# The short token set's first products moved into a long set's pass, with buffers and the pace of weight making laid out anew

## Chip, cores and metric

One core of a Trainium2 chip runs the whole program in one launch. The metric is the device time of one execution in microseconds (us); less is better. The engines: TensorE (PE in the rows; PEld is its weight load) multiplies, VectorE (DVE) and ScalarE (ACT) do elementwise work, GpSimd (POOL) a little of it, SyncE (SP) issues nearly all transfers. SBUF is the working memory, PSUM the eight banks of 512 float32 per partition that TensorE writes.

## What is computed

The reference, cut: kernel attention over 4 x 8 heads of 576 tokens, then two gated layers on the 2304 token rows of width 512, with a hidden width of 1536.

```python
def phi(x):
    h = np.einsum('bhsd,md->bhsm', x, omega) - np.sum(x * x, axis=-1, keepdims=True) / 2.0
    return np.exp(h - np.max(h, axis=-1, keepdims=True)) / np.sqrt(m)
q_p, k_p = phi(q * scale), phi(k * scale)
kv, z = np.einsum('bhsm,bhsd->bhmd', k_p, v), np.sum(k_p, axis=2)
x = np.einsum('bhsm,bhmd->bhsd', q_p, kv) / (np.einsum('bhsm,bhm->bhs', q_p, z)[..., None] + 1e-06)
x = x.transpose(0, 2, 1, 3).reshape(2304, 512)
g = x @ w_gate;  x = (g / (1 + np.exp(-g))) * (x @ w_val) @ w_out              # layer 1
x = (1 / (1 + np.exp(-(x @ w_gate2)))) * (x @ w_val2) @ w_out2                 # layer 2
```

The six layer weights come as float64 and are made float32 on the chip.

## The kernel before

**Attention** runs first (to about 165 us), pair of heads by pair, in an order written out by hand (`ORDER`). It leaves x transposed in `xx`: 512 features on partitions and blocks, 2304 tokens along the free axis. Of these 2048 are the long part (512 of each batch) and 256 the short one (`TAIL`, 64 of each batch).

**The layers.** Each layer handles three token sets: long set 0 and long set 1 of 1024 tokens (`big(l, n, ...)`), then the short set of 256 (`rest(l)`). A set has a first stage (x times w_gate and w_val, then the gate) and a second (hidden times w_out). Every product is three matmuls (`three`): each operand is split into a high and a low float32r part (xhi, xlo for x; vh, vl for a weight; hh, hl for the hidden values), the high part by a ScalarE copy, the low part by a VectorE subtraction.

**First stage of a long set.** The 12 hidden column blocks are done in 6 pairs `p`. A pair takes seven products in a Winograd form, `k` = 0 to 6, of the operands B11, T1, T2, B21, T3, B22, T4 (the T are differences of quarters of x, made by `x_sum`). Product k uses weight tile `w` of its slot, 12 matmuls of 512 columns, and lands in PSUM pair X, Z, X, Y, X, Z, X. X gathers k = 0, 2, 4 and 6 by accumulation, so that between them ScalarE copies it out (k = 0 and 2, `copy`), VectorE adds it to a temporary (k = 4, `total`, tiles p5 and u2), and after k = 6 `gate` reads it last. X alternates between two pairs of banks (`next_x`).

**Weights.** A unit (a 128 x 512 block) is loaded as float64 (raw), made float32 by one ScalarE operation (magnitude, L150) and four on VectorE (bits, power, term, total: L158 to L179), summed with its neighbours for the seven forms (`sums`, wsums, L224), and stored in DRAM (wf, ws). From there `fetch` reads each tile when its turn in `sequence` comes, three steps ahead (`AHEAD`), and `prepare` splits it (vh L314, vl L318). The 36 units of layer 1 must be made while attention and the first pass run: 12 are made inside attention (`early`), the others by the generator `make`, of which `step` takes a few turns after each product: as many as the weight `room` of that step and the next due time in `needs` ask for (`SHARES` scales this by stage).

**The short set** (`rest`) comes after the two long ones of its layer, with two weight tiles of two slots (0 and 3, or 6 and 7) for each hidden block, which it fetches and splits again, 24 tiles, and 12 of w_out: 36 tiles of 12 (layer 2's w_out: 6) matmuls each.

Engines run their own queues in order; waits are semaphores. TensorE's order in a long set's pair is the order of k, and behind it come the ready tile's steps. Lines that the text names: L261 `x_sum`, L271 and L274 `x_split` (xlo, xhi), L329 to L331 `three`, L870 and L871 `gate`, L878 and L879 `split` (hh, hl), L884 `copy`, L889 `total`, L896 `evict`.

Of the kernel before, what the change touches and what calls it, by code (L numbers as in the profile page):

```python
# [28 lines left out]
Q_ON_VECTOR = True  # L29
EARLY_SPLITS = 10  # L30
# [3 lines left out]
SHARES = (1, 1.5, 1, 1, 0.5), (1.2, 1.5, 1, 1, 1), 1  # L34
CALM = ()
MARGIN = 1
ENDS_BY = 1
NEGATIVE = -(2.0**32)
# [3 lines left out]
def tile_performer_attention__then__two_glu_layers(  # L42
# [170 lines left out]
    def sums(u, v, t):  # L213
# [17 lines left out]
        "T1": ("B12", "B11", 0),  # L231
        "T2": ("B22", "T1", 1),
        "T3": ("B22", "B12", 0),
        "T4": ("B21", "T2", 1),
    }
    xc, xt, fetched, ready = {}, {}, {}, {}
    sequence = []
    for l in range(2):
        for n in range(2):
            sequence += [("f", l, p, s) for p in range(FC // 2) for s in SLOT7]  # L240
            sequence += [("s", l, c) for c in range(FC)]
        for c in range(FC + 2):
            if c < FC:
                sequence += [("f", l, c // 2, s) for s in ((0, 3), (6, 7))[c % 2]]
            if c >= 2:
                sequence.append(("s", l, c - 2))

    def in_rest(o):
        return o % (len(sequence) // 2) >= 2 * (7 * FC // 2 + FC)

    def x_part(s, name):
        if name[0] == "T":
            return xt[name]
        k, ab = 2 * (name[1] == "2"), 2 * s + (name[2] == "2")
        return xx[:, k:k + 2, ab * TS:(ab + 1) * TS]

    def x_sum(s, name, later):
        l, r, place = SUMS[name]

        t = xt["T2"] if name == "T4" else temporary((("s0", "s1"), ("u2", "p5"))[later][place], "xt")  # L260
        nc.vector.tensor_tensor(t, x_part(s, l), x_part(s, r), ALU.subtract)  # L261
        xt[name] = t

    def x_split(s, i, low):
        k, kk = divmod(i, 2)
        tag = f"w{2 * RING + 2 * i + low}"
        t = wres.tile([P, TS], F32R, tag=tag, name="xlo" if low else "xhi")
        src = x_part(s, ORDER7[k])[:, kk]
        if low:
            hi = xc[k, kk][0]  # L270
            nc.vector.tensor_tensor(t, src, hi.bitcast(F32), ALU.subtract)  # L271
            xc[k, kk] = hi, t
        else:
            nc.scalar.activation(t, src, AF.Copy)  # L274
            xc[k, kk] = (t,)
# [15 lines left out]
    def fetch(o):  # L291
        if o < len(sequence) and o not in fetched and o not in ready:
            kind, l, c, *slot = sequence[o]
            if in_rest(o) and o % 6 > 3:
                t = temporary(("u2", "p5")[o % 2], "wp", shape=(P, 2 * H2))
# [3 lines left out]
            if kind == "s":  # L299
# [55 lines left out]
    with ExitStack() as st:  # L355
# [352 lines left out]
        early = [(n, units.pop(0)) for n in range(len(pairs) + 1) if n % 3 < 2]  # L708
# [9 lines left out]
        for (_, ua), (n, ub) in zip(early[::2], early[1::2]):  # L718
# [13 lines left out]
        def begin(i):  # L732
            if i == 0:
                begun.append(next_x())
# [33 lines left out]
    xs, tmp = pool("xs", 1), pool("tmp", 1)  # L768
    rows = out.rearrange("(b s) e -> b s e", s=S)
# [15 lines left out]
    def make():  # L785
# [3 lines left out]
        for _ in range(2):  # L789
            yield  # L790
# [39 lines left out]
    for at, (kind, l, *_) in enumerate(sequence):  # L830
        phase = at % (len(sequence) // 2)
        tail = phase >= 2 * 54
        share = SHARES[l][4 if tail else 2 * (phase // 54) + (phase % 54 >= 42)]
        if l == 0 and at < 7:
            share *= SHARES[2]
        if phase < 108 and phase % 54 in CALM:
            share *= 0.1
        room.append(share * (0.53 if tail else 1 + (kind == "s")))
    needs, turns = [], 3
# [12 lines left out]
    def step(n):  # L852
# [4 lines left out]
        prepare(o + AHEAD)  # L857
        o += 1
# [8 lines left out]
    def gate(l, h, src):  # L867
# [3 lines left out]
        after(1, lambda: nc.vector.tensor_tensor(h, g, src[1], ALU.mult))  # L871
# [14 lines left out]
    def total(l, h, left, t):  # L886

        for i in range(2):
# [217 lines left out]
```

## Time and profile before

| | |
|---|---|
| time, median of 3 runs | 1012.7 us (1012.38 to 1017.41) |
| the profiled execution | 1014.05 us, of which the span from first to last instruction is 1012.3 |
| PE busy | 989.5 us (98% of the span), 5497 matmuls |
| PEld, DVE, ACT, POOL busy | 844.2, 722.1, 595.8, 35.9 us |
| DMA | 167.54 MB moved, 53.1% of the engines' time in the queue that SyncE issues |

A busy matmul row lasts longer than the distance to the next one, since matmuls are pipelined; so the distance between starts is what counts, and idle time shows only where TensorE waited for something. Where VectorE or ScalarE is idle, nothing is lost unless TensorE waits for it later.

### The profile page before, as it was taken

What the parts mean: (1) busy time and instruction counts of PE and PEld (TensorE: products, weight loads), DVE (VectorE), ACT (ScalarE), POOL (GpSimd) and SP (SyncE); (2) the same over time, 40 slices, a digit from 0 to 9 for tenths busy, and PEclk for the clock granted to TensorE, in tenths of its full rate; (3) what the DMA queues carried; (4) which work ended last, traced back from release to release, by engine and by line L of the source; (5) the groups of instructions that cost most, each with busy time, mean ns of one, the idle gap of its engine ahead of it and who ended that gap; (6) DMA issues with size and microseconds to landing.
All of it is one profiled execution on the core that took longest, in us unless ns stands there. A gap on an engine that the chain in (4) does not pass through costs nothing.

```text
span 1012.3 us, 15829 instructions
## 1 busy us (share of the span) xinstructions
PE 989.5 (98%) x5497; PEld 844.2 (83%) x5497; DVE 722.1 (71%) x1465; ACT 595.8 (59%) x1259; POOL 35.9 (4%) x58
## 2 busy tenths in 40 slices
PE   7999999799999999999999999999999999999998
PEld 6999998588878888888789998888888888888897
DVE  6899998899988977678677757767553554553364
ACT  7999998455654465545456565565345545533454
POOL 2222220000000000000000000000000000000000
PEclk9999999799999999999999999999999999999999
DMA  7656866688875566665445666664114333321463
GB/s 211 166 155 171 219 178 184 193 281 295 276 228 156 158 202 182 189 188 176 132 126 186 218 206 206 204 192 143 52 53 136 102 96 92 105 55 50 166 197 96
DMA packets 136404, 167.54 MB, mean 166 GB/s; under 512 B 32260, under 2 KB 89604, under 8 KB 136324
## 3 DMA queue, kind: packets, MB, share of 16 engines
q1 hardware_dynamic: 134740, 163.65, 53.1%
q0 software_dynamic: 1584, 2.88, 1.7%
q8 instruction: 43, 0.70, 0.3%
q14 instruction: 37, 0.30, 0.1%
HBM read 127.43 MB, written 36.18 MB: 162 GB/s over the span
## 4 chain that ended last, share of the span: by engine, by line
PE 85%; DVE 7%; ACT 2%; issue 2%; DMA 1%; SPq 1%; DVEq 0%; ACTq 0%
PE X L329 14%; PE X L331 14%; PE X L330 14%; PE Z L329 6%; PE Z L331 6%; PE Z L330 6%; PE Y L331 5%; PE Y L329 5%; PE Y L330 5%; PE p L536 3%; PE o L590 2%; PE o L616 2%; PE o L602 1%; PE t L498 1%; DVE vl L318 1%
## 5 line engine op out<-in xcount | busy, mean ns | idle before, releaser
L318 DVE TENSOR_TENSOR vl<-wp,vh 128x512 fp32r<-128x512 f32 x288 | 197.5, 688 | 146.6 <-ACT vh L314 144.0
L314 ACT ACTIVATE vh<-wp 128x512 fp32r<-128x512 f32 x288 | 177.5, 623 | 14.2 <-PE Y L331 4.8
L329 PE MATMUL X<-xhi,vh 128*128 128x512 f32 x384 | 150.9, 393 | 7.4 <-DVE p L889 7.4
L330 PE MATMUL X<-xlo,vh 128*128 128x512 f32 x384 | 150.6, 392 | 0.3 <-DVE xlo L271 0.3
L331 PE MATMUL X<-xhi,vl 128*128 128x512 f32 x384 | 150.6, 392 | 0.0
L329 PEld LDWEIGHTS X<-xhi,vh 128*128 128x128 f32 x384 | 72.8, 190 | 23.1 <-issue 7.7
L879 DVE TENSOR_TENSOR hl<-h,hh 128x1024 fp32r<-128x1024 f32 (+1 forms) x56 | 49.3, 880 | 58.7 <-ACT hh L878 58.5
L330 PEld LDWEIGHTS X<-xlo,vh 128*128 128x128 f32 x384 | 72.8, 189 | 15.8 <-DVE xlo L271 0.7
L331 PEld LDWEIGHTS X<-xhi,vl 128*128 128x128 f32 x384 | 72.7, 189 | 15.4 <-DVE vl L318 0.2
L878 ACT ACTIVATE hh<-h 128x1024 fp32r<-128x1024 f32 (+1 forms) x56 | 43.5, 777 | 68.6 <-PE X L330 39.1
L329 PE MATMUL Z<-xhi,vh 128*128 128x512 f32 x192 | 75.0, 390 | 0.1
L330 PE MATMUL Z<-xlo,vh 128*128 128x512 f32 x192 | 74.8, 390 | 0.0
L331 PE MATMUL Z<-xhi,vl 128*128 128x512 f32 x192 | 74.8, 389 | 0.0
L331 PE MATMUL X<-xr,vl 128*128 128x256 f32 x192 | 54.3, 283 | 0.0
L329 PE MATMUL X<-xr,vh 128*128 128x256 f32 x192 | 54.2, 282 | 0.0
L330 PE MATMUL X<-xr,vh 128*128 128x256 f32 x192 | 54.2, 282 | 0.0
L150 ACT ACTIVATE mag<-raw 128x512 f32<-128x512 f32 x72 | 48.1, 673 | 6.7 <-DVE res L179 2.1
L171 DVE SCALAR_TENSOR_TENSOR mag<-raw,mag 128x512 f32<-128x512 uint32 x72 | 50.7, 704 | 1.2
L884 ACT ACTIVATE Y<-X 128x512 f32<-128x512 f32 x48 | 27.8, 584 | 35.9 <-PE X L331 35.4
L274 ACT ACTIVATE xhi<-xt 128x512 fp32r<-128x512 f32 x32 | 19.9, 630 | 47.2 <-DVE xt L261 47.2
L870 ACT ACTIVATE g<-u 128x512 f32<-128x512 f32 x24 | 15.2, 633 | 54.8 <-DVE u L889 54.8
L870 ACT ACTIVATE g<-p 128x512 f32<-128x512 f32 x24 | 15.2, 632 | 52.9 <-DVE p L889 52.9
(170 smaller groups left out, 2388.3 us busy)
## 6 DMA issues: line engine op xcount, KB each, us to landing
wp<-wf SPq DMA_DIRECT2D x216, 256.0 KB, 3.1
wp<-ws SPq DMA_DIRECT2D x72, 256.0 KB, 2.8
raw<-in_moe_w_gate_dram SPq DMA_DIRECT2D x24, 512.0 KB, 4.6
raw<-in_moe_w_val_dram SPq DMA_DIRECT2D x24, 512.0 KB, 4.8
wf<-res SPq DMA_DIRECT2D x48, 256.0 KB, 3.5
wf<-wsums SPq DMA_DIRECT2D x48, 256.0 KB, 3.6
raw<-in_moe_w_out_dram SPq DMA_DIRECT2D x24, 512.0 KB, 4.4
ws<-res SPq DMA_DIRECT2D x24, 256.0 KB, 3.8
```

Source lines behind the costliest of these rows:

```text
L150: nc.scalar.activation(self.mag, self.hi.bitcast(F32), AF.Prelu, scale=REBIAS, alpha=NEGATIVE)
L171: nc.vector.scalar_tensor_tensor(self.mag, self.lo, 2.0**-52, self.mag, ALU.mult, ALU.mult)
L314: nc.scalar.activation(hi, fetched[o], AF.Copy)
L318: nc.vector.tensor_tensor(lo, fetched.pop(o), hi.bitcast(F32), ALU.subtract)
L329: nc.tensor.matmul(o, lhsT=l[0], rhs=r[0], start=start, stop=False, **kw)
L330: nc.tensor.matmul(o, lhsT=l[0], rhs=r[1], start=False, stop=False, **kw)
L331: nc.tensor.matmul(o, lhsT=l[1], rhs=r[0], start=False, stop=stop, **kw)
L536: nc.tensor.matmul(pj[a][:, i, :], lhsT=x[hs, i, :], rhs=wdf[hs, a, :], start=True, stop=True)
L870: nc.scalar.activation(g, src[0], AF.Sigmoid if l else AF.Silu)
L878: nc.scalar.activation(hi, src, AF.Copy)
L879: nc.vector.tensor_tensor(lo, src, hi.bitcast(F32), ALU.subtract)
L884: nc.scalar.activation(d, s, AF.Copy)
```

## The change

`rest` is gone. The short set's first products run inside one long pass of each layer (layer 1: long set 0; layer 2: long set 1), on the weight tile that the step has in hand: `slots` marks slots 0, 3 and 7 of a pair as also used by the short set (12 matmuls of 256 columns more, `small_first`), and adds a step for slot 6, whose tile only the short set uses. In the pair p = 0 only slot 7 is shared, and slots 0, 3 and 6 follow as three steps of their own. So the program takes 256 weight tiles where it took 288; the number of matmuls stays. The short products land in a bank pair of their own (R, banks 4 and 5; one bank for both halves of a hidden block), and in these passes X stays on banks 0 and 1 instead of alternating. The short set's second products follow at once after that long set's second products.

SBUF: the temporaries p5 and u2 go; the copies of Z and X land in the hidden tiles themselves (h2, h1 and the next pair's h). The T differences live in the x operands' own tiles. The short set's split x and every second split of hidden blocks (hh, hl with odd c) share the tags xh and xl.

Weight making: a turn's room is now 2.74 times the step's products less 0.6 times an estimate of VectorE's work there, near nothing in the last slots of the last pair; the first 7 steps get a fifth; the last early pair's four sums move from attention into `make`. ScalarE's table loads for Silu and Sigmoid are asked for ahead by a one-element activation (`table`).

```diff
+LEAD = 3
+EARLY_UNITS = 12
+FULL = (4, 5, 6, None)
+SPENT = 0.6
+LEFT_OVER = 1
-SHARES = (1, 1.5, 1, 1, 0.5), (1.2, 1.5, 1, 1, 1), 1
+SHARES = ((1, 1, 1, 1), (1, 1, 1, 1), 0.2, 7)
+LATE_START = (7,)
+SMALL_AT = 7
...
+    LARGE = (0, 0, True), (0, 1, False), (1, 0, False), (1, 1, True)
+    REST = {0: (0, 0), 3: (0, 1), 7: (1, 1), 6: (1, 0)}
+    def slots(l, n, small, p):
+        ks = [(s, k, small and s in REST) for k, s in enumerate(SLOT7)]
+        if small and p == 0:
+            ks = [(s, k, s in LATE_START) for s, k, _ in ks]
+            return ks + [(s, None, True) for s in (0, 3, 7, 6) if s not in LATE_START]
+        return ks + [(6, None, True)] * small
...
+                full = p == FC // 2 - 1 and product in FULL
+                vector.append(9 if full else 0.6 + {4: 1.8, 5: 1.8, 6: 0.6, None: 0.6}.get(product, 0))
...
+        left_over = [(a[1], b[1]) for a, b in couples[len(couples) - LEFT_OVER:]]
...
-        room.append(share * (0.53 if tail else 1 + (kind == "s")))
+        room.append(share * max(2.74 * x - SPENT * y, 0.1))
...
         prepare(o + AHEAD)
+        while soon:
+            soon.pop(0)()
...
-            temporary(f"s{2 * low + c % 2}", "h" + "hl"[low], F32R, src.shape)
+            temporary((f"s{low}", "x" + "hl"[low])[c % 2], "h" + "hl"[low], F32R, src.shape)
...
+    def table(f):
+        nc.scalar.activation(tiny[:, 1:], tiny[:, :1], f)
...
+    def small_first(kh, w, bank, start, stop):
+        for n in range(2):
+            for kk in range(2):
+                fs = slice(n * H2 + kk * P, n * H2 + (kk + 1) * P)
+                three(
+                    bank[:, n * R:(n + 1) * R],
+                    [u[:, fs] for u in w],
+                    [u[:, 2 * kh + kk] for u in small_x],
...
-            X, Y = begun or (next_x(), banks(3, "Y"))
+            X, Y = begun or (banks(0, "X") if small else next_x(), banks(3, "Y"))
...
+                if r and k == 0:
+                    small_step()
...
                 if k == 1:
-                    copy([p5[:, i] for i in range(2)], Z)
+                    copy(h2, Z)
+                    if early:
+                        table(AF.Silu)
                 if k == 2:
-                    copy([u2[:, i] for i in range(2)], X)
+                    h[2 * p + 2] = h_tile(2 * p + 2)
+                    u2 = h[2 * p + 2][:, 0] if p < FC // 2 - 1 else h[2 * p + 2][0]
+                    u2 = [u2, h1[1]]
+                    copy(u2, X)
...
                 if k == 6:
-                    after(1, partial(gate, l, h2[0], X))
+                    after(1, partial(gate, l, h2[0], X, small))
+                if r and k != 0:
+                    small_step()
...
-                    hs[c] = split(h[c], c)
+                    after(1 + (c == 0), partial(lambda c: hs.update({c: split(h[c], c)}), c))
+        if small:
+            acc = [ps.tile([P, MAIN], F32, tag=f"b{i}", name="acc") for i in (6, 7, 2, 3, 4, 0, 1, 5)]
...
+            elif small and c + 2 == FC:
+                small_hi_lo(0)
...
-        rest(0)
```

**How the order moves: three places.** VectorE's queue in pair p = 0 of the first pass, before, from the low split of slot 4's tile (vl) to the adds after k = 4. In the names, res and mag are a unit being made, xt the T difference (here T4), X and p5 the PSUM pair and the temporary of `total`.

```order
L318 TENSOR_TENSOR vl_3224<-wp_2917,vh_3223 128x512
L171 SCALAR_TENSOR_TENSOR mag_3196<-raw64_3172,mag_3196 128x512
L179 TENSOR_TENSOR res_3198<-res_3198,mag_3196 128x512
L158 TENSOR_SCALAR res_3235<-mag_3233 128x512
L261 TENSOR_TENSOR xt_2471<-xx_76,xt_2471 128x1024
L271 TENSOR_TENSOR xlo_3252<-xt_2471,xhi_3250 128x512
L271 TENSOR_TENSOR xlo_3256<-xt_2471,xhi_3254 128x512
L318 TENSOR_TENSOR vl_3261<-wp_3170,vh_3260 128x512
L165 TENSOR_SCALAR mag_3233<-res_3235 128x512
L171 SCALAR_TENSOR_TENSOR mag_3233<-raw64_3174,mag_3233 128x512
L179 TENSOR_TENSOR res_3235<-res_3235,mag_3233 128x512
L158 TENSOR_SCALAR res_3273<-mag_3271 128x512
```

The same stretch of the change, from two xlo ahead of slot 3's tile to the adds; h stands where p5 stood.

```order
L304 TENSOR_TENSOR xlo_3123<-xt_3068,xhi_3109 128x512
L304 TENSOR_TENSOR xlo_3135<-xt_3068,xhi_3121 128x512
L352 TENSOR_TENSOR vl_3165<-wp_2555,vh_3164 128x512
L352 TENSOR_TENSOR vl_3186<-wp_2738,vh_3185 128x512
L230 TENSOR_TENSOR wsums_3195<-res_3074 128x256
L304 TENSOR_TENSOR xlo_3215<-xx_76,xhi_3213 128x512
L304 TENSOR_TENSOR xlo_3219<-xx_76,xhi_3217 128x512
L352 TENSOR_TENSOR vl_3222<-wp_2919,vh_3221 128x512
L295 TENSOR_TENSOR xt_2472<-xx_76,xt_2472 128x512 x2
L304 TENSOR_TENSOR xlo_3243<-xt_2472,xhi_3241 128x512
L304 TENSOR_TENSOR xlo_3247<-xt_2472,xhi_3245 128x512
L352 TENSOR_TENSOR vl_3252<-wp_3168,vh_3251 128x512
```

The res and mag rows are gone from this stretch (five ahead of T4, four behind), three of four wsums have moved behind it, and slot 3's vl now stands behind two xlo that it preceded.

VectorE's queue at the end of the first pass (pair p = 5), before, from the adds after k = 5 to the last gate product, which frees the pair X.

```order
L889 TENSOR_TENSOR u2_4181<-Z_4180,u2_4181 128x512
L871 TENSOR_TENSOR xx_76<-g_4307,p5_4182 128x512
L318 TENSOR_TENSOR vl_4336<-wp_4256,vh_4335 128x512
L171 SCALAR_TENSOR_TENSOR mag_4285<-raw64_4231,mag_4285 128x512
L179 TENSOR_TENSOR res_4315<-res_4315,mag_4285 128x512
L879 TENSOR_TENSOR hl_4348<-h_3163,hh_4347 128x1024
L871 TENSOR_TENSOR xx_76<-g_4333,u2_4181 128x512
L318 TENSOR_TENSOR vl_4368<-wp_4279,vh_4367 128x512
L158 TENSOR_SCALAR res_4373<-mag_4345 128x512
L165 TENSOR_SCALAR mag_4345<-res_4373 128x512
L171 SCALAR_TENSOR_TENSOR mag_4345<-raw64_4281,mag_4345 128x512
L871 TENSOR_TENSOR xx_76<-g_4365,X_4176 128x512
```

The same of the change.

```order
L939 TENSOR_TENSOR xx_76<-Z_4515,xx_76 128x512
L929 TENSOR_TENSOR hl_4695<-h_3158,hh_4694 128x1024
L915 TENSOR_TENSOR xx_76<-g_4672,xx_76 128x512
L352 TENSOR_TENSOR vl_4702<-wp_4603,vh_4701 128x512
L915 TENSOR_TENSOR xx_76<-g_4699,xx_76 128x512
L929 TENSOR_TENSOR hl_4733<-h_3159,hh_4732 128x1024
L352 TENSOR_TENSOR vl_4739<-wp_4644,vh_4738 128x512
L915 TENSOR_TENSOR xx_76<-g_4736,X_4511 128x512
L352 TENSOR_TENSOR vl_4761<-wp_4678,vh_4760 128x512
L915 TENSOR_TENSOR hr_4757<-g_4758,R_4517 128x256
```

No res or mag row stands there any more; both hl stand ahead of the product that frees X, and behind it comes the short set's last gate product, which frees R.

ScalarE's queue at the same place of the change, from the gate after k = 5.

```order
L912 ACTIVATE g_4699<-u2_4596 128x512
L348 ACTIVATE vh_4701<-wp_4603 128x512
L928 ACTIVATE hh_4732<-h_3159 128x1024
L912 ACTIVATE g_4736<-X_4510 128x512
L348 ACTIVATE vh_4738<-wp_4644 128x512
L912 ACTIVATE g_4758<-R_4517 128x256
L348 ACTIVATE vh_4760<-wp_4678 128x512
```

hh_4732 takes over the memory of the short set's split x (tag xh), so that it waits for TensorE's last short product of the pass, and the gate on X now stands behind it.

## Rows read from the trace of the kernel before

**Rows 1.** which engine TensorE waited for, whole span: us in total, times, longest
```profile
PE X L329 <- DVE p L889: 7.4, 1, 7.4
PE X L329 <- DVE xx L871: 2.6, 2, 2.4
```

**Rows 2.** stages: busy us (x instructions) of PE, PEld, DVE, ACT, POOL; clock, DMA
```profile
183.30:195.90 12.60, 5.26 (x13) 4.14 (x14) 10.02 (x18) 7.00 (x12) 0.00 (x0) 0.60 0.42 125
195.90:291.20 95.30, 95.30 (x422) 78.93 (x421) 90.48 (x170) 56.62 (x102) 0.00 (x0) 1.00 0.85 275
...
362.20:476.40 114.20, 114.20 (x505) 94.62 (x504) 81.41 (x146) 64.42 (x115) 0.00 (x0) 1.00 0.60 182
...
543.80:595.40 51.60, 51.60 (x434) 51.57 (x433) 36.28 (x72) 31.02 (x66) 0.00 (x0) 1.00 0.76 247
595.40:956.40 361.00, 361.00 (x1586) 297.42 (x1585) 199.78 (x301) 179.00 (x298) 0.00 (x0) 1.00 0.39 117
```

**Rows 3.** timeline of TensorE, pair p = 0: start us, us, what [idle before]
```profile
175.15 0.50 PE L331 MATMUL Y<-xhi,vl 128*128 128x512 f32 x1 [0.25 <-DVE vl L318]
...
182.89 0.39 PE L331 MATMUL Z<-xhi,vl 128*128 128x512 f32 x1
190.63 0.76 PE L329 MATMUL X<-xhi,vh 128*128 128x512 f32 x1 [7.35 <-DVE p L889]
...
195.89 0.44 PE L329 MATMUL X<-xhi,vh 128*128 128x512 f32 x1
```

**Rows 4.** timeline of VectorE, pair p = 0
```profile
174.41 0.68 DVE L318 TENSOR_TENSOR vl<-wp,vh 128x512 fp32r<-128x512 f32 x1
175.01 0.42 DVE L224 TENSOR_TENSOR wsums<-wsums,res 128x256 f32<-128x256 f32 x1
175.35 0.68 DVE L271 TENSOR_TENSOR xlo<-xt,xhi 128x512 fp32r<-128x512 f32 x1
...
177.83 0.42 DVE L158 TENSOR_SCALAR res<-mag 128x512 uint32<-128x512 uint32 x1
...
178.62 1.28 DVE L271 TENSOR_TENSOR xlo<-xx,xhi 128x512 fp32r<-128x512 f32 x2
...
182.09 1.22 DVE L261 TENSOR_TENSOR xt<-xx,xt 128x1024 f32<-128x1024 f32 x1
184.00 1.29 DVE L271 TENSOR_TENSOR xlo<-xt,xhi 128x512 fp32r<-128x512 f32 x2 [0.69 <-ACT xhi L274]
186.95 0.69 DVE L318 TENSOR_TENSOR vl<-wp,vh 128x512 fp32r<-128x512 f32 x1 [1.65 <-ACT vh L314]
...
189.80 1.29 DVE L889 TENSOR_TENSOR p<-X,p 128x512 f32<-128x512 f32 x2
```

**Rows 5.** timeline of ScalarE, pair p = 0
```profile
173.34 0.68 ACT L150 ACTIVATE mag<-raw 128x512 f32<-128x512 f32 x1
...
183.34 1.15 ACT L274 ACTIVATE xhi<-xt 128x512 fp32r<-128x512 f32 x2 [6.13 <-DVE xt L261]
184.51 1.28 ACT L870 ACT_TABLE_LOAD   x1
185.80 0.60 ACT L870 ACTIVATE g<-Y 128x512 f32<-128x512 f32 x1
```

**Rows 6.** timeline of TensorE, end of the first pass
```profile
295.83 0.40 PE L331 MATMUL X<-hh,vl 128*128 128x512 f32 x1
298.62 0.80 PE L329 MATMUL X<-hh,vh 128*128 128x512 f32 x1 [2.39 <-DVE xx L871]
...
301.77 0.42 PE L330 MATMUL X<-hl,vh 128*128 128x512 f32 x1
```

**Rows 7.** timeline of VectorE, end of the first pass
```profile
294.02 1.22 DVE L879 TENSOR_TENSOR hl<-h,hh 128x1024 fp32r<-128x1024 f32 x1
...
297.88 0.68 DVE L871 TENSOR_TENSOR xx<-g,X 128x512 f32<-128x512 f32 x1
```

**Rows 8.** timeline of ScalarE, end of the first pass
```profile
292.52 1.04 ACT L878 ACTIVATE hh<-h 128x1024 fp32r<-128x1024 f32 x1
```

More of the change, by code (lines that the diff above doesn't have):

```diff
@@ L273, in x_split @@
         else:
+            t = wres.tile([P, TS], F32R, tag=x_tag(k, kk, 0), name="xhi")
             nc.scalar.activation(t, src, AF.Copy)
@@ L707, in tile_performer_attention__then__two_glu_layers @@
         }
-        early = [(n, units.pop(0)) for n in range(len(pairs) + 1) if n % 3 < 2]
+        early = [n for n in range(len(pairs) + 1) if n % 3 < 2][:EARLY_UNITS]
+        early = [(n, units.pop(0)) for n in early]
         for name in "load", "magnitude", "bits", "power", "term", "total":
@@ L768, in tile_performer_attention__then__two_glu_layers @@
     xs, tmp = pool("xs", 1), pool("tmp", 1)
+    tiny = tmp.tile([P, 2], F32, name="tiny")
+    nc.vector.memset(tiny, 0.0)
     rows = out.rearrange("(b s) e -> b s e", s=S)
@@ L788, in make @@
             u.load()
-        for _ in range(2):
-            yield
+        for u, v in left_over:
+            t = []
+            yield from sums(u, v, t)
+            put(u, v, t)
         todo = None
@@ L829, in tile_performer_attention__then__two_glu_layers @@
     room = []
[L830 to L834, printed above, removed]
+    for (kind, l, *_), x, y in zip(sequence, weight, vector):
+        second = sum(z[0] == "s" and z[1] == l for z in sequence[:len(room)]) >= FC
+        share = SHARES[l][2 * second + (kind != "f")]
+        if len(room) < SHARES[3]:
             share *= SHARES[2]
-        if phase < 108 and phase % 54 in CALM:
-            share *= 0.1
-        room.append(share * (0.53 if tail else 1 + (kind == "s")))
-    needs, turns = [], 3
+        room.append(share * max(2.74 * x - SPENT * y, 0.1))
+    needs, turns = [], 1 + 4 * LEFT_OVER
     for i, u in enumerate(units):
@@ L886, in total @@
     def total(l, h, left, t):
-        for i in range(2):
-            nc.vector.tensor_tensor(t[:, i], left[i], t[:, i], ALU.add)
-        after(1, lambda: gate(l, h, [t[:, i] for i in range(2)]))
+        for x, y in zip(left, t):
+            nc.vector.tensor_tensor(y, x, y, ALU.add)
+        after(1, lambda: gate(l, h, t))
+    def table(f):
+        nc.scalar.activation(tiny[:, 1:], tiny[:, :1], f)
     def evict(n, dst, src):
@@ L902, in big @@
         own = slice(n * 2 * TS, (n + 1) * 2 * TS)
+        if small:
+            held = [tmp.tile([P, i, R], F32, tag=f"hr{at}", name="hr") for at, i in enumerate(HELD[:-1])]
         def h_tile(c):
+            if c == FC:
+                return [wres.tile([P, TS], F32, tag=x_tag(0, 0, 0), name="u2")]
             if c < 8:
@@ L942, in big, with small_hi_lo @@
                     c = (k - 3) // 2
-                    hs[c] = split(h[c], c)
-        acc = [next_x(), banks(3, "Y"), banks(1, "Z"), next_x()]
-        acc = [t for pair in acc for t in pair]
+                    after(1 + (c == 0), partial(lambda c: hs.update({c: split(h[c], c)}), c))
+        if small:
+            acc = [*Y, *Z, R2[0], *X, R2[1]]
+            acc = [ps.tile([P, MAIN], F32, tag=f"b{i}", name="acc") for i in (6, 7, 2, 3, 4, 0, 1, 5)]
+        else:
+            acc = [t for pair in (next_x(), banks(3, "Y"), banks(1, "Z"), next_x()) for t in pair]
         todo = [f for _, f in following]
-        for _ in range(2):
+        for _ in range(3):
             clock += 1
             run()
+        if l == 0 and n == 1:
+            table(AF.Sigmoid)
+        hr = {}
+        def small_hi_lo(i):
+            hr[i] = split(held[i], i)
         for c in range(FC):
@@ L973, in big @@
             store(dst, t[:, b % 2])
[L975 to L992 removed]
+        if not small:
+            return
         Y = banks(3, "Y")
         acc = [t[:, j * R:(j + 1) * R] for t in Y for j in range(2)] if l == 0 else Y
[L995 to L1005 removed]
         def second(c, w, js=range(4 - 2 * l)):
+            i, at = place_of(c)
+            now = [u[:, at] for u in hr[i]]
             for j in js:
```

213 lines of the change are left out of this document (114 added, 99 removed).

## The prediction, made before the changed kernel ran

> **What bounds the kernel now.** First the stages, to see which engine is full in each: TensorE is busy for all of 195.9 to 291.2, 362.2 to 476.4, 543.8 to 595.4 and 595.4 to 956.4 [rows 2]. There its own pace sets the time, and what other engines save is worth nothing. That pace is the distance between starts: 114.2 us for the 504 matmuls of a long first stage, 0.2267 us each at 512 columns (one row of the 505 is the next stage's), and 51.6 for 434 in the short set, 0.119 each at 256 [rows 2]. Then the list of who waits: in the layers TensorE waited 7.4 us once for the adds on X, and 2.6 us twice for the gate product on X, the longer time 2.4, so the other 0.2 [rows 1]. Third, the timeline at both places. At the first the next matmul starts at 190.63 instead of 183.12, and then the next twelve start 0.44 apart on average, not 0.2267, until 195.89 [rows 3]: the granted clock of 183.3 to 195.9 is 0.60 [rows 2], that is, 1.2 GHz for part of it and not 2.4. At the second it starts at 298.62 instead of 296.06, again with the lower clock behind it, until 301.77 [rows 6]. All that can be won in the layers is there: 7.5 + 2.5 and 2.6 + 1.6, and 0.2, some 14.4 us.
>
> **Why TensorE waits at 183.** X is freed by the adds at 189.80. VectorE was never idle before T4's difference at 182.09: it had the weight making, the sums and the splits to do in order [rows 4]. T4 ended at 183.3; then came ScalarE's high splits, a table load of 1.28, a gate, slot 6's vh [rows 5], and VectorE's xlo, vl (late at 186.95), four making operations, the adds [rows 4].
>
> **The change, step by step.** The sum is made against the profiled execution, 1014.05 us with a span of 1012.3; the median of the runs is 1012.7, and I take the difference from that.
>
> *Matmuls: 0.* Their number and shapes stay. 576 short products cost 0.119 each before, and I take the same when they alternate with long ones; the bounds are half a long one's 0.2267, 0.0057 less, which is -3.3 us, and as much more, +3.3.
>
> *32 weight tiles fewer: 0.* Transfer, vh and vl of the short set lie under TensorE, which is busy for all 51.6 us of its stage [rows 2]; VectorE there has 36.3. Without that cover a tile would cost VectorE the 0.69 of a vl [rows 4].
>
> *Opening (p = 0).* Ahead of T4 VectorE loses five making operations: 177.83 to 182.09 is 4.26, less an xlo pair 1.2 and a vl 0.6 that stay, 2.45; and three of four sums, 0.34 each (175.01 to 175.35), 1.0 [rows 4]. It gains some 0.1 for a memset and a second instruction of T4. So T4 ends at 183.3 - 3.35 = 179.95. Then the high splits (0.55 each), the gate on Y and slot 6's vh (0.5 each) take ScalarE to 181.7 with no table load between [rows 5]; vl ends at 182.3, one sum at 182.65, the first add at 183.25, the second at 183.85. One step gets later: slot 3's vl, for which TensorE waited 0.25 at 175.15 [rows 3], now stands behind two xlo (+1.2) and one sum fewer (-0.35) and the memset (+0.1): TensorE stops 1.2 instead of 0.25 and ends k = 5 at 184.05 instead of 183.12. Then X is free and k = 6 goes at once, 12 x 0.2267 = 2.7, done at 186.8 where it was 195.89 [rows 3]: **-9.1**. The table load moves to k = 1, where ScalarE loses two magnitude operations of 0.68 [rows 5] for its 1.28: 0 net, and slot 5's splits hide it. Bounds: none of the lower clock, or 1.2 us of idle time calling it for as long as 2.4 did [rows 6], 1.6 lost; or the fall of 3.35 alone helps, the first rival.
>
> The load took 1.28 us, and the next activation began 0.01 after it [rows 5]. The Trainium skill (ScalarE: Activation LUTs, "What ACT_TABLE_LOAD costs") says that a switch costs some 2.66 us, since 1.38 of draining comes on top of the load; the trace does not agree. By the page slot 5's splits and T4 would come about 1 us later in the new place, and the sum below would be -12.0.
>
> *Pair 0 to 1.* The three added steps last 12 x 0.119 = 1.43 each, and pair 1 begins with a short product on R, whose gate and product come only a step earlier. VectorE's queue from the adds on (two xr, seven splits, adds and gate products at 0.6, two sums) brings R free at about 192.7; TensorE is there at 192.5. **+0.3**; 0 to 1.2 (a gate product and a vl more).
>
> *The rest of the first pass.* VectorE was busy 90.5 of 95.3 us there [rows 2], nearly full. Now the stage has 24 uses of 12 short products, 34 us more of TensorE, for at most 15 us of VectorE (8 vl, 12 gate products, a split of x): 0.
>
> *End of a short-carrying pass.* Before, 2.6 + 1.6 were lost here, because the product that frees X stood behind making operations and an hl [rows 7]. The making is gone from the stretch. A new wait comes: hh_4732 waits for the last short product, and behind it on ScalarE stand the gate on X and on R, on VectorE hl, vl and both products. From that product's end: hh 1.04, hl 1.2, vl 0.6, product 0.6 and hand-overs [rows 4, 7, 8], some 3.6. The second products begin on six other banks' worth, so that X's second bank is wanted after 6 x 3 x 0.2267 = 4.1, R's after 4.8, and R comes 4.7 to 4.9 after. **-4.1** for layer 1's old stop, **+0.2** for both layers together; 0 to 1.0.
>
> *Short second stage.* The third hh takes the place of the first, so it waits for product 3; hh, hl and vl need at most 2.9 before product 6, and products 4 and 5 give 2.9. **+0.1**, 0 to 0.6. Stores and the end stay as they were.
>
> *Second pass, layer 1.* Little making is left in its last slots either: **-0.2** of the 0.2.
>
> Sum: -9.1 + 0.3 - 4.1 + 0.2 + 0.1 - 0.2 = -12.8. The profiled execution would take 1001.3, and the median 1012.7 - 12.8 = **999.9 us**.
>
> **The rivals.**
>
> *The opening is only shortened.* If the chain behind T4 keeps its length (a late transfer, another operation ahead of the adds), only the 3.35 of T4 is won, the idle time stays at 4 us and the lower clock with it: -3.35 - 4.1 + 0.3 = 1005.5. For it: the chain had two other waits, on vh and xhi [rows 4]. Against it: table load and four making operations leave the chain too.
>
> *Slower: one pair X.* In the short-carrying passes X no longer alternates, so k = 0 of the next pair waits for the gate product after k = 6. From X's last matmul there are 2 x 1.43 of short products, 1.43 more ahead of k = 0, and 1.36 for X's first bank: 5.65. Before, at the end of the first pass, that product ended at 298.5, 7.3 after 291.2 [rows 2, 7]. Were it as late at each of ten boundaries, each would cost 1.65 and some lower clock, as much again: 33, less the 12.8, so 1033. It decides from 1.3 a boundary. Against it: the chain itself is 0.5 + 0.6 + 0.6, the lateness was making's, and in layer 2's pass VectorE is little loaded (199.8 of 361 [rows 2]).
>
> *No change: given back later.* The first 7 steps make a fifth as much, and pair 3's tiles wait for their units; the 12.8 returns as stops for a tile: 1012. Against it: the first pass's 34 us against 15 above.
>
> **How the numbers follow.** The forecast, with the bounds of its terms, 0.70; the opening only shortened 0.13; one pair X, 0.08; given back 0.05; better than the forecast's bounds 0.04. The bounds of the forecast: -3.3 at most below, and above 1.6 + 0.9 + 0.8 + 0.5, so 996.6 to 1003.7. The range takes in the first rival and some room above it, 996.5 to 1008, and leaves out about 0.15. Half a per cent is 5 us, about what a measurement here tells from no change: below 1007.6 lie the forecast, what is better and most of the first rival, 0.85; within, the rest of it and the giving back, 0.07; above 1017.8 the single X, 0.08.
>
> **What the profile would show.** Right: in pair 0 TensorE stops near 176 for about a microsecond and not at 183, and the granted clock stays at its upper level; at most a fraction of a microsecond at the first short product of pair 1 and at the gate products at the end of both short-carrying passes; weight splits 256 and not 288; starts 0.119 apart for short products between long ones. Wrong: TensorE idle ahead of k = 0 of several pairs for a gate product on X (the slower rival); idle for vl or vh of a later pair (given back); a stop of some 4 us for the adds in pair 0 (only shortened).

## The result, and the profile after

The changed kernel took 1004.85 us, the median of five runs (1003.85 to 1007.74), beside 1014.47 of the kernel before on the same chip (1012.38 to 1017.41): a ratio of 0.9909, 95% interval 0.9883 to 0.9935. So 9.6 us were won where 12.8 were forecast. The time lies inside the range, but 1.2 us above the 996.6 to 1003.7 that the forecast's own terms allowed, in part because the kernel before took 1014.47 here and not 1012.7; as a difference, 9.6 lies near the low end of what the terms allowed, 9.0 to 16.1. The number alone does not tell the forecast from the first rival, "only shortened" (1005.5): the timelines below do. The profiled execution took 1003.85 us with a span of 1002.1, 10.2 less than before.

First who waits for whom on TensorE in the layers (us in total, times, longest), beside [rows 1]:

```profile
PE R L363 <- DVE hr L915: 1.6, 2, 0.8
PE Y L365 <- DVE vl L352: 1.1, 1, 1.1
PE X L364 <- DVE xlo L304: 0.4, 1, 0.4
```

The wait of 7.4 and the two that made up 2.6 are gone. Now the stages by windows of the changed kernel (columns as in [rows 2]): pair 0, the rest of the short-carrying first stage, its second products, the short set's second products; then in layer 2 the plain pass's second products, the carrying first stage, and all that follows it.

```profile
166.87:186.55 19.68, 18.20 (x80) 14.12 (x78) 19.18 (x37) 14.35 (x27) 0.86 (x1) 1.00 0.49 147
186.55:316.86 130.31, 129.52 (x710) 112.45 (x708) 111.55 (x211) 69.64 (x128) 0.00 (x0) 1.00 0.78 244
316.86:384.01 67.15, 67.15 (x290) 53.98 (x289) 56.83 (x92) 35.57 (x56) 0.00 (x0) 1.00 0.54 170
384.01:401.15 17.14, 17.14 (x145) 17.14 (x144) 14.23 (x26) 11.17 (x22) 0.00 (x0) 1.00 0.66 206
...
696.86:764.16 67.30, 67.30 (x289) 54.18 (x288) 36.51 (x49) 29.91 (x45) 0.00 (x0) 1.00 0.22 69
764.16:913.31 149.15, 148.36 (x794) 128.32 (x793) 67.29 (x109) 67.60 (x123) 0.00 (x0) 1.00 0.32 93
913.31:997.60 84.29, 84.29 (x362) 67.50 (x360) 32.35 (x40) 32.61 (x49) 0.00 (x0) 1.00 0.27 85
```

The stages of the kernel before that [rows 2] did not part (layer 1's first second products, then layer 2's three last stages):

```profile
291.19:362.17 70.98, 68.59 (x290) 55.10 (x289) 60.95 (x97) 35.17 (x57) 0.00 (x0) 0.98 0.58 179
...
709.66:775.91 66.25, 66.25 (x290) 54.07 (x288) 35.23 (x44) 29.23 (x44) 0.00 (x0) 1.00 0.22 68
775.91:890.16 114.25, 114.25 (x505) 94.63 (x504) 58.17 (x89) 60.07 (x106) 0.00 (x0) 1.00 0.35 104
890.16:1007.16 117.00, 117.00 (x649) 101.76 (x647) 53.15 (x84) 50.28 (x90) 0.00 (x0) 1.00 0.37 115
```

The granted clock is 1.00 in every row of after (0.60 at the old stop, [rows 2]), and VectorE in the rest of the first stage has fallen from 95% busy to 111.55 of 130.31 (86%). TensorE's timeline in pair 0, beside [rows 3]: two stops, none at k = 6, whose first matmul goes 0.23 after the one ahead of it, and then the stop at pair 1's first short product.

```profile
172.30 0.50 PE L364 MATMUL X<-xlo,vh 128*128 128x512 f32 x1 [0.36 <-DVE xlo L304]
...
175.98 0.50 PE L365 MATMUL Y<-xhi,vl 128*128 128x512 f32 x1 [1.12 <-DVE vl L352]
...
183.60 0.39 PE L365 MATMUL Z<-xhi,vl 128*128 128x512 f32 x1
183.83 0.39 PE L363 MATMUL X<-xhi,vh 128*128 128x512 f32 x1
...
186.55 0.28 PE L363 MATMUL R<-xr,vh 128*128 128x256 f32 x1
...
193.10 0.36 PE L363 MATMUL R<-xr,vh 128*128 128x256 f32 x1 [0.79 <-DVE hr L915]
```

VectorE's timeline there, beside [rows 4]: T4's difference, the adds on X for which TensorE used to wait, and further on the gate product that frees R, behind a vl.

```profile
178.59 1.28 DVE L295 TENSOR_TENSOR xt<-xx,xt 128x512 f32<-128x512 f32 x2
...
182.64 1.29 DVE L939 TENSOR_TENSOR h<-X,h 128x512 f32<-128x512 f32 x2
...
191.94 0.69 DVE L352 TENSOR_TENSOR vl<-wp,vh 128x512 fp32r<-128x512 f32 x1
192.55 0.41 DVE L915 TENSOR_TENSOR hr<-g,R 128x256 f32<-128x256 f32 x1
```

### The profile page after: what moved, and what is told of

It reads as the page before. It is cut to its first block, busy times and chain, and to the rows that moved or that the text cites. A ratio compares the mean times of both kernels' runs of the same rounds, so it can differ in the third digit from the quotient of the medians.

```text
span 1002.1 us, 15606 instructions
## 1 busy us (share of the span) xinstructions
PE 987.1 (99%) x5497; PEld 839.9 (84%) x5497; DVE 702.1 (70%) x1436; ACT 577.0 (58%) x1215; POOL 36.0 (4%) x58
## 4 chain that ended last, share of the span: by engine, by line
PE 93%; DVE 3%; ACT 2%; SPq 1%; issue 1%; DMA 0%; ACTq 0%
PE X L363 11%; PE X L364 11%; PE X L365 11%; PE Z L363 5%; PE Z L365 5%; PE Z L364 5%; PE acc L363 4%; PE acc L364 4%; PE acc L365 4%; PE Y L365 4%; PE Y L364 4%; PE Y L363 4%; PE p L570 3%; PE o L624 2%; PE R L363 2%; PE R L364 2%
## 5 line engine op out<-in xcount | busy, mean ns | idle before, releaser
L352 DVE TENSOR_TENSOR vl<-wp,vh 128x512 fp32r<-128x512 f32 x256 | 175.4, 688 | 155.3 <-ACT vh L348 153.2
L348 ACT ACTIVATE vh<-wp 128x512 fp32r<-128x512 f32 x256 | 158.2, 622 | 4.2 <-DMA wp<-wf 1.3
L929 DVE TENSOR_TENSOR hl<-h,hh 128x1024 fp32r<-128x1024 f32 x32 | 39.2, 1224 | 54.7 <-ACT hh L928 54.7
L928 ACT ACTIVATE hh<-h 128x1024 fp32r<-128x1024 f32 x32 | 33.8, 1057 | 66.8 <-PE acc L364 22.6
L363 PE MATMUL R<-xr,vh 128*128 128x256 f32 x192 | 53.7, 280 | 1.6 <-DVE hr L915 1.6
L365 PE MATMUL R<-xr,vl 128*128 128x256 f32 x192 | 53.5, 279 | 0.0
L364 PE MATMUL R<-xr,vh 128*128 128x256 f32 x192 | 53.5, 279 | 0.0
L912 ACT ACTIVATE g<-h 128x512 f32<-128x512 f32 x28 | 17.8, 635 | 59.3 <-DVE h L939 59.3
L185 DVE TENSOR_TENSOR res<-res,mag 128x512 f32<-128x512 f32 x61 | 42.0, 688 | 1.1
L928 ACT ACTIVATE hh<-xx 128x1024 fp32r<-128x1024 f32 x16 | 17.0, 1060 | 44.4 <-PE acc L364 16.1
```

What stands on the lines that cost most here:

```text
L185: nc.vector.tensor_tensor(self.res, self.res, self.mag, ALU.add)
L348: nc.scalar.activation(hi, fetched[o], AF.Copy)
L352: nc.vector.tensor_tensor(lo, fetched.pop(o), hi.bitcast(F32), ALU.subtract)
L363: nc.tensor.matmul(o, lhsT=l[0], rhs=r[0], start=start, stop=False, **kw)
L364: nc.tensor.matmul(o, lhsT=l[0], rhs=r[1], start=False, stop=False, **kw)
L365: nc.tensor.matmul(o, lhsT=l[1], rhs=r[0], start=False, stop=stop, **kw)
```

## The experiments

Theory: the gain is the opening and the end of the carrying pass, and what carries it in layer 1 is the TensorE time of the short products, under which VectorE makes weights. Rivals: the calmer pace of weight making does it alone; or details of the same diff do (the moved sums, the early table load, the rule for the last slots). Where a kernel has one run and it lies between the 1003.85 and 1007.74 of the changed kernel, its time says nothing and its stops are what counts.

**The pace without the moved products** (e1_before_pace). The kernel before, with a fifth of the making in its first 7 steps and little at the end of a pass:

```diff
-SHARES = (1, 1.5, 1, 1, 0.5), (1.2, 1.5, 1, 1, 1), 1
-CALM = ()
+SHARES = (1, 1.5, 1, 1, 0.5), (1.2, 1.5, 1, 1, 1), 0.2
+CALM = (38, 39, 40, 41)
```

> The kernel before, with the short set left in its own stage, and two numbers of its pace alone changed: the first seven steps make a fifth as many weights, and the last pair's last four steps a tenth. If the pace is what won (my theory): the stop of 7.5 us in the first pair falls to some 2.5 us, since the making is gone from VectorE's queue there and only the table load and three sums stay, with 0 to 1.6 us of lower clock behind it; the stop of 2.6 us and the 1.6 us behind it at the first pass's end go; the span falls by 8 to 10 us of 1012.3, as far as the change did. If moving the short products is what won, since only their time relieves VectorE: the making comes back as stops in later pairs and the span falls by less than 4 us.

Measured: 1016.69 us (ten runs), ratio 1.0029 (1.0011 to 1.0047). Its TensorE timeline shows where the making went, into pairs that had no stop before:

```profile
225.07 0.50 PE L331 MATMUL Z<-xhi,vl 128*128 128x512 f32 x1 [0.46 <-DVE vl L318]
229.23 0.47 PE L329 MATMUL X<-xhi,vh 128*128 128x512 f32 x1 [1.59 <-DVE p L889]
...
247.21 0.50 PE L329 MATMUL X<-xhi,vh 128*128 128x512 f32 x1 [2.83 <-ACT u L884]
```

The stop at k = 6 shrank from 7.35 to 2.81 and the one at the pass's end to 0.4, as the theory of the pace had it, but all of it came back later. So the pace alone wins nothing: the making that it puts off needs time. Not only VectorE's: the longest of the stops that came back, 2.83, is the copy out of X on ScalarE, which stood behind the first operation of a unit whose load had not landed:

```profile
246.00 0.67 ACT L150 ACTIVATE mag<-raw 128x512 f32<-128x512 f32 x1 [5.89 <-DMA raw<-in_moe_w_val_dram]
246.57 1.07 ACT L884 ACTIVATE u<-X 128x512 f32<-128x512 f32 x2
```

**The short products' time taken away** (e9_short_third). Of each short first product two of three matmuls are left out (the parts with a low half), so that TensorE has 22.4 us less to do in each carrying pass while VectorE and ScalarE do the same:

```diff
-                three(
+                nc.tensor.matmul(
...
-                    [u[:, fs] for u in w],
-                    [u[:, 2 * kh + kk] for u in small_x],
+                    lhsT=w[0][:, fs],
+                    rhs=small_x[0][:, 2 * kh + kk],
```

> The changed kernel with two of the three matmuls of each short first product left out (the short set's result then lacks its low parts), so that TensorE has 288 x 0.1167 = 33.6/3 x 2 = 22.4 us less to do in the carrying pass of each layer, and VectorE and ScalarE do exactly what they did. If it is the short products' time that lets VectorE make the weights in layer 1's first pass (what the pace run now points to): stops of TensorE come back in that pass, 4 to 12 us in all, and the pass gets only 10 to 18 us shorter; in layer 2, where nothing is made, the pass gets shorter by the whole 22.4, within 1 us. If VectorE's order alone is what counts: both passes get 22.4 shorter and no new stop is over 0.5 us.

Measured: 982.04 us (one run). Counted from the first xlo stop to the end of layer 1's carrying first stage, 144.6 us became 141.3 (174.02 to 315.29), 3.3 shorter of 22.4; layer 2's carrying first stage 149.15 became 127.8, 21.3 shorter. The rest went into waits, nearly all in layer 1, and into the lower clock behind two of them (0.71 from 194.78 to 200.00, 0.79 from 238 to 246):

```profile
PE R L974 <- ACT vh L348: 5.1, 5, 1.9
PE R L974 <- DVE hr L915: 2.9, 1, 2.9
PE X L363 <- DVE h L939: 2.8, 2, 1.8
PE X L363 <- DVE h L915: 2.3, 3, 1.5
```

The theory's direction is shown, and layer 2 came within about its 1 us; for layer 1 it had said 10 to 18 us shorter with stops of 4 to 12, and the measured 3.3 is far less, so the cover counts for more than it had. In layer 1 the short products run in time that VectorE, ScalarE and the loads need anyway, in layer 2 they do not. The last row is the wait of the slower rival (the gate product on X, one pair of banks); it is there only when this cover is thin.

**The start at full pace** (e2_full_start). `SHARES[2]` 0.2 becomes 1.

> The changed kernel with the first seven steps making weights at the full rate again. If the fifth in the first seven steps is what cut the opening: making operations come back ahead of T4's adds, 2 to 3 us of VectorE, and TensorE stops 1.5 to 4 us at k = 6, with the lower clock behind it, span 2 to 6 us longer. If the sums and the table load moved out of the way were enough: a stop under 0.5 us more, span within 1 us.

Measured: 1012.73 us (one run), with a span of 1011.0, 8.9 longer where 2 to 6 were expected. The stop at k = 6 is back at 2.7, with the lower clock behind it (0.50 from 187.54 to 190.50), and R's first release, which the expectation did not have, is 3.1 late:

```profile
PE R L363 <- DVE hr L915: 3.9, 2, 3.1
PE X L363 <- DVE h L939: 2.7, 1, 2.7
```

So the pace is needed as well: with the moved products it costs nothing later, without them it does.

**The last early sums back in attention** (e10_no_left_over). `make` then has these turns fewer, so that the next unit's operations come sooner.

```diff
-LEFT_OVER = 1
+LEFT_OVER = 0
```

> The changed kernel with the last couple of the start's left-over units put back ahead of the token split, as in the kernel before (the constant of that name 0 instead of 1): slot 3's low weight part is then made ahead of two of the X parts' low halves, and the sums of the opening come later. If the opening's two stops are the price of the order in which VectorE hands out low parts, the stop of 1.1 us at slot 3's low part shrinks below 0.4, and the time of two sums and two low halves on VectorE (3 to 5 us, against 2.3 us that the stops of 0.4 and 1.1 let it fall behind) shows as stops of 2 to 5 us in all at the X parts or at k = 4 of the first pair. Rival: the short products' cover takes it, all stops of the first pair together stay at 1.5 us or less and the time is that of the changed kernel.

Measured: 1018.86 us (one run). The stop for slot 3's vl fell from 1.12 to 0.23, as the order says. The price was expected at k = 4 as well, but as 2 to 5 us of VectorE's work; it was 5.87 and a load's. ScalarE stood at the first magnitude operation of the next unit, whose load had been issued at 177.27 and had not landed, and behind it stood the copy out of X that k = 4 waits for (ScalarE, then TensorE):

```profile
182.49 0.66 ACT L156 ACTIVATE mag<-raw 128x512 f32<-128x512 f32 x1 [7.62 <-DMA raw<-in_moe_w_gate_dram]
183.05 1.08 ACT L934 ACTIVATE h<-X 128x512 f32<-128x512 f32 x2
```

```profile
183.69 0.79 PE L363 MATMUL X<-xhi,vh 128*128 128x512 f32 x1 [5.87 <-ACT h L934]
```

The lower clock followed (0.51 from 183.69 to 188.92), and VectorE's making, late by then, cost stops of 0.5 to 3.0 in pairs 1 to 3. In the changed kernel the same load is issued at 176.34 and its magnitude stands at 193.20, so that nobody waits. The sums' place and the sooner turns, which share this constant, weren't parted.

**The rule for the last slots** (e3_no_full). `FULL = ()`: the making goes on in the last pair's last steps.

> The changed kernel with the last pair's last slots making weights as the others do. If keeping the making out of them is what took away the stop at the first pass's end: a stop of 0.5 to 2.5 us for the gate product on X or on R at the start of the second products. If the short products behind k = 6 cover it anyway: under 0.3 us.

Measured: 1007.14 us (one run), with a new stop at the pass's end: the second products on R's bank wait 1.5 for the last gate product. Another of 0.66 stands at the adds in pair 2. No stop for X came back at the pass's end.

```profile
PE acc L363 <- DVE hr L915: 1.5, 1, 1.5
```

**No early table load** (e4_no_table). `table` does nothing; the first gate loads the table itself.

> The changed kernel without the early table loads: each comes ahead of the first gate of its kind, as before. If the forecast's step is right: slot 6's vl and the adds come 1.28 us later, X is free at about 184.6 and TensorE stops some 0.5 us at k = 6 of pair 0; layer 2's load costs nothing. If the load is hidden: no stop there. By the price with draining (the Trainium skill, ScalarE: Activation LUTs, What ACT_TABLE_LOAD costs) the stop would be 1.9 us.

Measured: 1006.53 us (one run). At k = 6 of pair 0 TensorE stops 0.92 (0.5 was expected, 1.9 by the price with draining), in pair 1 vh comes 0.98 late and the adds of a later pair 0.7; in layer 2 nothing changes.

```profile
PE X L363 <- DVE h L939: 1.6, 2, 0.9
PE R L363 <- ACT vh L348: 1.0, 1, 1.0
```

So asking ahead is worth some 1.8 us in layer 1 (0.92 + 0.98 + 0.71, less the 0.79 of R's stop there, which is gone).

**Pair 1's first short product put behind its long one** (e5_short_second), to remove R's stop:

```diff
-                if r and k == 0:
+                if r and k == 0 and p != 1:
...
-                if r and k != 0:
+                if r and (k != 0 or p == 1):
```

> The changed kernel, but in pair 1 of a short-carrying pass the short product of slot 0 comes behind the long one of that slot and not ahead of it. If R's late release by the gate product of pair 0 is the whole of the two stops of 0.95 us between pair 0 and 1 (my theory): both stops go, -1.9 us, as X has been free for four steps. If X's single pair is as late as R (rival): TensorE stops there for X, and nothing is won.

Measured: 1006.69 us (one run, in which attention ended 2.8 us later). Both R stops are gone, but layer 1 has two new ones, for the adds of k = 4 in pairs 1 and 2:

```profile
PE X L363 <- DVE h L939: 1.6, 2, 1.4
```

From the first xlo stop to the end both kernels take 829.8 us. VectorE is at its edge in this pass, so a stop that is taken away at one place returns at the next.

**Where the operands lie** (e6_align). Second products go 0.2333 us apart after the change, first products 0.2267. Two tiles made larger move the split activations (hh, hl, and the short set's xr) by 32 bytes to multiples of 64:

```diff
-    tiny = tmp.tile([P, 2], F32, name="tiny")
+    tiny = tmp.tile([P, 16], F32, name="tiny")
+    pad = late.tile([P, 8], F32, name="pad")
+    nc.vector.memset(pad, 0.0)
```

> The changed kernel with two pads of SBUF alone (the one-element tile for the table loads takes 64 bytes and not 32, and 32 bytes are left at the top of memory), so that hh and hl, the split x of the short set and the weight buffers begin at multiples of 64 bytes as the operands of the first products do. After the change the second products of long sets start 0.2333 us apart and those of the first 0.2267; before the change it was 0.230 to 0.232, with hh off by 32 bytes and hl not. If the operands' addresses set the distance: second products at 0.2267, 1152 of them, -7.6 us, span about 994.5. If it is the change of bank after each three matmuls or which operand is stationary: 0.2333 as it was, span 1002 within 0.5.

Measured: 1002.78 us (four runs), ratio 0.9882 (0.9857 to 0.9906). Layer 1's second products gain 1.2 us in each pass, layer 2's 0.1. So the place counts, but the expected 0.2267 was reached in neither layer (the same stages as after the change, by windows):

```profile
318.61:384.61 66.00, 66.00 (x291) 54.02 (x290) 56.55 (x92) 35.44 (x56) 0.00 (x0) 1.00 0.53 173
384.61:401.57 16.96, 16.96 (x146) 16.96 (x145) 14.32 (x27) 11.23 (x21) 0.00 (x0) 1.00 0.66 205
696.06:763.25 67.19, 67.19 (x289) 54.14 (x288) 36.54 (x49) 29.90 (x45) 0.00 (x0) 1.00 0.20 69
912.80:996.96 84.16, 84.16 (x362) 67.42 (x360) 32.37 (x40) 32.60 (x49) 0.00 (x0) 1.00 0.27 85
```

**High and low parts apart** (e7_high_apart), with these pads: the high ones in one pair of tiles and the low ones in the other, as before the change:

```diff
-            temporary((f"s{low}", "x" + "hl"[low])[c % 2], "h" + "hl"[low], F32R, src.shape)
+            temporary((f"s{c % 2}", "x" + "hl"[c % 2])[low], "h" + "hl"[low], F32R, src.shape)
```

> The padded kernel with the tags of the hidden blocks' splits exchanged: both high parts lie in the upper memory (where they lay before the change) and both low parts in the other, which adds a wait at the start of the second products, since the first low part waits for the short set. Its start distances are what counts. If where hh and hl lie against each other sets the distance of layer 2's second products: 0.230 us there, as in the kernel before, and not 0.2333 as in the changed and the padded one. If it is something else: 0.2333.

Measured: 1010.11 us (one run). The distances stay, 0.229 in layer 1 and 0.2333 in layer 2, and at the ends of the carrying passes hl and vl come up to 2.4 us late, since the split of hidden blocks now waits for another tile. Which tile holds which part isn't the cause.

**Pads and exchange together**, in both layers, and in layer 2 alone (there `p != 1` becomes `p != 1 or l == 0`, and `p == 1` becomes `p == 1 and l == 1`):

> The changed kernel with the padded operands of e6_align and, in the second pair of columns of both carrying passes, slot 0's short product behind the long one, as in e5_short_second. Theory that the two edits act apart: the two stops of 0.8 to 1.0 us at the release of the short bank (one in each layer) go, as in e5_short_second; the stops of 0.3 and 1.5 us at the adds of slot 3's sum in layer 1's second pair come as there; so layer 1 gains nothing and layer 2 about 1 us: 1001.5 to 1003 us median against 1002.8 of e6_align. Rival (the stops of layer 1 only changed place by that execution's late attention): layer 1 gains too and the time is 1000.5 to 1001.5.

> As e8_align_second, but with the exchange in layer 2 alone. Where layer 1 only trades one stop for another, this run keeps layer 1's stop of 0.8 to 1.0 us on the release of the short bank near 193 us of the span, has none in the second pair of layer 2's carrying pass, and takes 1001.3 to 1002.3 us median: 0.5 to 1.0 below e6_align's 1002.8, and as fast as e8_align_second or up to 1 us faster. By the rival it is about 1 us slower than e8_align_second. In both, layer 2's second products keep their start distance of 0.2333.

Measured: 1003.20 us (five runs; ratio 0.9880, 0.9861 to 0.9900) and 1002.09 us (four runs; 0.9875, 0.9856 to 0.9894). With the exchange in both, layer 1 has the stop for the adds again, and longer than the one that it replaced:

```profile
PE X L363 <- DVE h L941: 1.7, 1, 1.7
```

With it in layer 2 alone, layer 1 keeps R's stop and layer 2 has none. The theory holds in the traces; by the times the two kernels and e6_align are not parted, their intervals overlap.

**All split activations at multiples of 128 bytes** (e12_align_128). The kernel with the exchange in layer 2, and larger pads:

```diff
-    tiny = tmp.tile([P, 16], F32, name="tiny")
-    pad = late.tile([P, 8], F32, name="pad")
+    tiny = tmp.tile([P, 32], F32, name="tiny")
+    pad = late.tile([P, 24], F32, name="pad")
```

> As e11_align_layer2, with the pads made larger, so that all split activations and the split of the short set begin at multiples of 128 bytes and not only of 64. Before the change the second products' high parts began 96 bytes past such a multiple and the low parts on one (0.2300 apart in layer 2, 0.232 in layer 1); after it all began 32 or 96 past (0.2333 in both); in e6_align all 64 past (0.229 in layer 1, 0.2333 in layer 2); the first products' operands, all on one, go 0.2267 apart. Theory that the start distance hangs on the place within 128 bytes: layer 1's second products 0.2267 apart (66.0 us becomes 65.3 for each of two passes), layer 2's 0.2267 to 0.230 (67.2 becomes 65.3 to 66.2, and the last pass as much), in all 3 to 5 us below e11_align_layer2's 1002.1: 997 to 999.2 us median. Rival, that layer 2's distance has another cause: 0.2333 stays there, layer 1 gains 0 to 1.4, and the time is 1000.7 to 1002.1.

Measured: 1001.94 us (four runs), ratio 0.9870 (0.9851 to 0.9889), the lowest median of all, though by the intervals it is not parted from e6_align or the two kernels with the exchange. By windows, the same four stages:

```profile
318.29:384.69 66.40, 66.40 (x290) 54.00 (x289) 56.62 (x91) 35.53 (x56) 0.00 (x0) 1.00 0.55 171
384.69:401.88 17.19, 17.19 (x146) 17.18 (x145) 14.43 (x26) 11.34 (x22) 0.00 (x0) 1.00 0.64 205
696.67:762.94 66.27, 66.27 (x290) 54.18 (x289) 36.53 (x49) 29.93 (x45) 0.00 (x0) 1.00 0.23 70
912.18:995.32 83.14, 83.14 (x362) 67.44 (x360) 32.37 (x40) 32.62 (x49) 0.00 (x0) 1.00 0.27 86
```

The mechanism was half right: layer 2 has the distance of before again, 66.27 for 66.25, and 1.0 less in the last stage. But layer 1 lost 0.4 against e6_align, and the products of 256 columns went from 0.1178 to 0.1196, 1.3 us over 720. So the time is what the rival gave.

## Why the prediction was right, and where its sizes were off

The balance of the layers, start to start, with the 288 short first products of a carrying pass (0.1167 each, 33.6 us) counted with the short set; each difference is after less before, and the last stage ends with the start of the last matmul (1007.16, now 997.20).

| step | forecast | measured | from |
|---|---|---|---|
| opening, to the end of k = 6 | -9.1 | -9.2 | 166.98 to 195.89; 166.87 to 186.55 |
| pair 0 to 1 and rest of the first stage | +0.3 | +1.4 | 95.30; 130.31 - 33.6 = 96.7 |
| layer 1's carrying second products | -4.1 + 0.1 | -3.8 | 70.98; 67.15 |
| short set of layer 1 | +0.1 | -0.8 | 51.54; 17.14 + 33.6 |
| second pass, layer 1 | -0.2 | -0.2 | 67.38; 67.16 |
| layer 2, plain pass, second products | 0 | +1.05 | 66.25; 67.30 |
| layer 2, carrying pass, all | +0.1 | +1.8 | 231.25; 233.04 |
| sum | -12.8 | -9.8 | |

The rest of the span's 10.2 lies outside: attention ended 0.1 sooner, and the end behind the last matmul is 0.2 shorter.

**The opening** went as worked out: T4's difference ended at 179.87 (179.95 forecast), slot 3's vl cost 1.12 (1.2), the adds were done in time, k = 6 ended at 186.55 (186.8). The start at full pace and the two runs on order and table show how little room it has: each of the three edits taken back brings a stop of its own.

**The first stage's cover** held. VectorE's work there grew by 21.1 us (90.48 to 111.55) and not by at most 15; in the opening it fell by 7.0 (26.19 to 19.18), so that making put off by the calmer start accounts for most of the difference. That 34 us of TensorE pay for it is what the run with a third of the short matmuls shows, and the pace run that the calmer pace without them wins nothing. Of the stage's +1.4, 0.95 is R's release, below; the rest is spread over the starts of the long products there. **The slower rival** (one pair X) and **given back later** did not come; **only shortened** had the right mechanism, an operation or a transfer ahead of the adds, and it is what the run without the moved sums shows, at k = 4 and not at k = 6.

**The end of the pass** came without a stop. The 2.6 + 1.6 of [rows 1, 6] were 3.84 in the stage (70.98 less the 67.14 of TensorE's busy time in the next pass): the term was 0.3 too large. Two things changed there, the making gone from the last slots and the short products behind k = 6, and either goes far alone: without the short products (the pace run) the stop on X fell from 2.39 to 0.40, and with the making back in these slots there was none on X, but 1.5 on R.

**What was mis-sized: R's release.** The prediction took it for a matter of VectorE's load and counted it in layer 1 only, +0.3. It cost 0.95 in each layer (a start 1.07 after the last one instead of 0.12; the rows' idle time is 0.79), and the longer reading of the bound, "a gate product and a vl more", was the right one. Layer 2, where VectorE was idle, shows that it is a fixed chain (ScalarE, then VectorE, then TensorE):

```profile
787.66 0.39 ACT L912 ACTIVATE g<-R 128x256 f32<-128x256 f32 x1 [2.33 <-PE R L365]
787.94 0.62 ACT L348 ACTIVATE vh<-wp 128x512 fp32r<-128x512 f32 x1
```

```profile
788.60 0.69 DVE L352 TENSOR_TENSOR vl<-wp,vh 128x512 fp32r<-128x512 f32 x1 [2.54 <-ACT vh L348]
789.20 0.41 DVE L915 TENSOR_TENSOR hr<-g,R 128x256 f32<-128x256 f32 x1
```

```profile
789.76 0.36 PE L363 MATMUL R<-xr,vh 128*128 128x256 f32 x1 [0.79 <-DVE hr L915]
```

The gate on R is done at 788.05, but its product stands behind a vl that waits for a vh which ScalarE makes after that gate: 0.6 + 0.6 later. That the product ahead of this vl would remove the stop was not tried.

**What was left out: the distance of starts.** "Matmuls: 0" held for number and shape. The distances moved: shorts 0.1192 to 0.1167, -0.7 a layer; layer 2's second products 0.2300 to 0.2337, +1.05 in the plain pass and some 1.3 in the carrying one (360 of them). With R's 0.95, 0.25 for the carrying pass's first products (0.2272 for 0.2267, 504 of them) and -0.7, that is the +1.8 of the last row. The forecast's bounds for shorts, -3.3 to +3.3, hold this; for second products it had none.

## What to carry to other kernels

Work that shares an operand saves its second preparation, but here it won because it put 34 us of the bounding engine's time where the making of weights (loads, ScalarE, VectorE) was behind; ask where a moved product's time lands before asking what it saves. A pace table that calms one place moves the load to the next unless such time is added. When a product behind a semaphore frees a bank, follow the chain on both engines word for word even where they are idle: a fixed order, not load, set the stop on R.

## What the runs showed of the hardware

The distance between matmul starts changed with the place in SBUF where the split activations begin. Of the tiles that TensorE reads in these stages, only these change their place within 128 bytes between the four programs; the split weights and the long sets' split x begin at multiples of 128 in all. Distances in us, from the rows above and the same stages of the other runs:

| bytes past a multiple of 128 (compiled program) | short first, 256 columns | layer 1 second | layer 2 second |
|---|---|---|---|
| before: hh 96, hl 0, xr 0 | 0.1192 to 0.1196 | 0.2331 | 0.2300 |
| after: hh and hl 96 or 32, xr 32 | 0.1167 | 0.2332 | 0.2337 |
| e6_align: all 64 | 0.1178 | 0.229 | 0.2333 |
| e12_align_128: all 0 | 0.1196 | 0.2301 to 0.2306 | 0.2301 |

That the pads change the distance is shown by two pairs of programs that differ in them alone: after and e6_align, e11_align_layer2 (as e6_align in this table) and e12_align_128. The same pads also move tiles that TensorE does not read here (the unsplit weight wp, the gated hidden values hr); that these have no part was not shown. A rule isn't shown either: no place is best for all three, and 0.2267, which the first products have with every operand on a multiple of 128, was reached by none. The kinds also differ in the activation's part: in the short first and layer 1's second products it is the operand whose columns stream (written first in the rows, `R<-xr,vh` and `acc<-hh,vh`), in layer 2's second products the loaded one (`acc<-vh,hh`); whether that is why they differ was not tested. A layout with a place for each kind was not tried.
